# Part of the gate work moved to GpSimd, first loads issued before a branch, and the third weight slice stored as high and low halves

## The chip, the cores and the metric

One core of a Trainium2 chip runs the program. The metric is the device time of one execution in microseconds (us), given as the median of several runs. The engines are TensorE (PE; its weight loads are shown apart as PEld), VectorE (DVE), ScalarE (ACT), GpSimd (POOL) and SyncE (SP, which here only issues DMAs).

## The reference

An mLSTM attention layer (4 batches, 8 heads, 768 steps, 40 values a head) is followed by a feed-forward layer with a rational activation:

```python
m_new = maximum(f + m, i);  f_stab = exp(f + m - m_new);  i_stab = exp(i - m_new)
C = f_stab * C + i_stab * outer(v, k);   n = f_stab * n + i_stab * k
y = sigmoid(o) * (C @ q) / maximum(abs(n . q), 1)          # step by step over 768 steps
x = y as (3072 tokens, 320)
h = x @ w_in                                               # 320 x 2048
P = a0 + a1*h + a2*h^2 + a3*h^3;  Q = 1 + |b0|*|h| + |b1|*h^2
out = (P / (Q + 1e-6)) @ w_out                             # 2048 x 320
```

The weights arrive as float64; everything else is float32.

## The kernel before

**Stages.** The attention is cut into 24 units (`u`) of 128 steps of one batch. Two units give 256 tokens of x, one block (`n`); there are 12 blocks. Each block is multiplied with `w_in`, goes through the activation and is multiplied with `w_out` in 8 feed-forward units (`i`). So that the first weights are enough for some work, the first two blocks are done by halves: units 0 to 3 of both, then 4 to 7 of both.

**Weights.** They come as pairs of 32-bit integers and are decoded on the chip (`split64`, L732), in slices: i0 to i7 (rows 0 to 255 of `w_in`, 512 KB each), o0 to o7 (`w_out`, 640 KB each), and j0, j1 (rows 256 to 319 of `w_in`, the third slice). A slice takes a load on SP (`raw`), a fill of `lo` and a rebase of `z` on ACT, two integer steps on DVE (a sign step and a join, one pair for each slice i or j), a cast to the high half on ACT, and a subtraction on POOL that leaves the low half. The feed-forward matmuls are products of high and low halves: 8 matmuls of 256 columns make one 128-row chunk of h (`f_f1`, tile `ph`), and 12 of 320 columns make a piece of the second product (tile `po`).

**The third slice** has only 64 rows, so its matmul uses two 64-row halves at once. Tile `wj` holds the high half in one set of partitions, and a DMA (`across`, L826, 4 x 128 KB) copies it into the others. Tile `wY` has the low half in partitions 0 to 63 and zeros in 64 to 127, put there by a memset of 64x2048 on POOL. The x tile `xk` has in its fifth part the high half of the last 64 columns of x in the first partitions and the low half in the others.

**Gates.** Before the first unit a small exponential (`early`) gives the first gates. For all later ones, `gate_m` is a running maximum (a scan on DVE), `gate_f` gets it added (32x512, DVE), eight subtractions of 32x128 give `gate_x` (four on POOL, "li", four on DVE, "lx"), and a row of DVE steps of 128x256 (tiles `gate_x` and `gP`) makes the exponential. `squares` (five steps of 128x1 on DVE) prepares the constants of the activation. For each unit, `e` is a scan (DVE), `kp`, `pm` and `tm` are products on POOL, `ab` and `kT` copies on ACT, `qA` a product of 104x512 (on DVE for the first ten units, on POOL afterwards), and `sm` the new state (for the first of each batch a plain copy, on DVE).

**The order.** All steps stand in one list, written out by hand (`ORDER`, L147 on). Each engine's instructions are chained in that order (`_Queue`, L34, so every such instruction shows L34 in the profile); SP's DMAs are chained likewise, and each DMA waits for the one 8 before it. "hot" are 90 matmuls of the identity with itself whose result nobody reads; each shows as two matmuls in the trace. What runs ahead of the list is `_prologue`: it loads a 4-value tensor and decides on it (`_can_square`, `_decide`), and the program branches on that number, so that nothing of the list starts before it.

```python
parts = [
    (w[:, 0, 0], 0), (w[:, 1, 0], 0), (w[:, 0, 1], 1), (w[:, 1, 1], 1),
    (w[:, 0, 0], 2), (w[:, 0, 1], 3), (wX, 4), (wY[:, c * P : (c + 1) * P], 4),
]
```

Of the kernel before, what the change touches and what calls it, by code (L numbers as in the profile page):

```python
# [147 lines left out]
early early.1 le early.2 early.3 hot hot.1 hot.2 hot.3 hot.4 hot.5 hot.6 hot.7 hot.8 hot.9 hot.10 hot.11 hot.12 hot.13  # L148
hot.14 hot.15 hot.16 hot.17 raw_o1 s2_o1 early.4 zero early.5 early.6 early.7 early.8 early.9 early.10 s0_o1.1
early.11 mc early.12 early.13 early.14 early.15 early.16 early.17 eye1 early.20 early.21 gate.2 gate.4 gate.5 li.2 eye  # L150
s0_o1 s1_o1 s3_o1 li.1 hot.18 s1_o1.1 s3_o1.1 lk_0 pf_0 early.18 raw_i6 gate.6 sc_0 hot.19 hot.20 hot.21 raw_o0 hot.22
pa_0 hot.23 s2_i6 hot.24 hot.25 hot.26 hot.27 s2_o0 s0_o0 o0_o1 s1_o0 hot.28 hot.29 zero.2 s3_o0 s0_o0.1 pa_1 s1_o0.1
s3_o0.1 li.3 lv_0 raw_j1 o2_o1 s0_i6 hot.30 hot.31 hot.32 early.19 ogl_4 gate.3 hot.33 hot.34 ogl_2 s1_i6 squares lx.2
raw_i4 o0_o0 hot.35 hot.36 s0_i4 s2_i4 pc_0 kp_0 tk_0 ke_0 pc_1 s0_j1 s1_i4 o2_o0 hot.37 hot.38 zero.3 s3_i4 o0_i4
ek_0 hot.39 hot.40 hot.41 hot.42 hot.43 zero.1 hot.44 hot.45 hot.46 hot.47 lq_0 hot.48 hot.49 hot.50 raw_o5 hot.51
hot.52 hot.53 hot.54 hot.55 hot.56 o2_i4 hot.57 hot.58 hot.59 hot.60 hot.61 s2_j1 s1_j1 s3_i6 raw_i2 lk_1 raw_j0 s0_o5
kp_1 li s3_j1 ogl_0 o0_i6 s0_o5.1 lq_1 s1_o5 lx.1 hot.62 tq_0 hot.63 s2_o5 eq_0 s1_o5.1 hot.64 o0_j1 hot.65 hot.66
pa_2 ogl_3 o2_i6 lx.3 s3_o5.1 s3_o5 o0_o5 S_0 tk_1 hot.67 qa_0 P_0 P_0.1 lx s0_j0 pc_2 ogl_5 raw_i0 ow_0 pf_1 gate.7
u0_0 ek_1 gate.21 lv_1 hot.68 tq_1 s1_j0 o2_j1 hot.69 hot.70 hot.71 d1_0 ogl_1 lk_2 o2_j1.1 sc_1 s2_j0 s3_j0 eq_1
s0_i2 hot.72 hot.73 hot.74 s2_i2 hot.75 S_1 ke_1 qa_1 o2_o5 o0_j0 o2_j0 raw_i3 u1_0 P_1 s1_i2 P_1.1 hot.76 pf_2 s0_i0  # L160
s1_i0 raw_i1 s2_i0 og_0 o2_j0.1 gate.1 ow_1 gate s3_i2 it_0 s3_i0 u0_1 d1_1 it_0.1 i1_0 hot.77 ab_0 ab_0.1 lq_2 hot.78
hot.79 hot.80 hot.81 sc_2 s0_i3 rc_0 kp_2 u1_1 s1_i3 tk_2 hot.82 g_0 x_0 o0_i0 o0_i2 g_0.1 ke_2 s2_i3 s3_i3 x_0.1
hot.83 hot.84 hot.85 hot.86 hot.87 hot.88 hot.89 ek_2 s2_i1 pf_3 s0_i1 s1_i1 s3_i1 xt_0 o2_i0 oc_j0 xh_0 xl_0 tq_2
eq_2 xh_0.1 o0_i1 o0_i3 S_2 lk_3 xl_0.1 raw_o3 lv_2 kp_3 tk_3 f1_0_0 f1_0_0.1 P_2 P_2.1 ek_3 s0_o3 s2_o3 o2_i1 lf_4
lq_3 ow_2 qa_2 sc_3 o2_i2 ha_0_0 s1_o3 s0_o3.1 pa_3 s3_o3 u0_2 d1_2 ke_3 u_0_0 s1_o3.1 s3_o3.1 p1_0_0 p3_0_0 u1_2
w_0_0 tq_3 eq_3 S_3 P_3 y_0_0 r0_0_0 P_3.1 lk_4 f1_0_1 sc_4 kp_4 tk_4 pc_3 raw_o2 gh_0_0 ek_4 m_0_0 oc_j1 f1_0_1.1
f1_0_2 qa_3 s0_o2 s0_o2.1 raw_i7 rm_0_0 s1_o2 s2_o2 ha_0_1 o2_i3 u_0_1 s1_o2.1 p1_0_1 s0_i7 s3_o2 s2_i7 w_0_1 gl_0_0
# [1306 lines left out]
```

## Time and profile before

| | us |
|---|---|
| median of 3 runs | 500.86 |
| the three runs | 499.60, 500.86, 504.22 |
| the profiled execution | 500.23 |
| its span (first to last instruction) | 498.4 |
| time around the span | 1.8 |
| TensorE's granted clock over the span, as a share of full speed | 0.998 |

The profile is of one execution. Its span is what the views of the trace cut up: a page by engine, tables by stretch of time, groups of instructions, waits, the single engines' timelines, and DMA issues. The part around the span is not seen in them.

### The profile page before, as it was taken

The page shows a single profiled execution, that of the slowest core. Times are in us where ns is not written, and L with a number is a line of the kernel's source. Part 1 is how long each engine was busy: PE and PEld are TensorE (multiplying, and loading weights), DVE is VectorE, ACT ScalarE, POOL GpSimd, SP SyncE. Part 2 cuts the span into 40 slices and gives each one's busy share as a digit, 9 for nine tenths or more (in the row PEclk, how much of TensorE's full clock was granted, in tenths as well). Part 3 has the DMA queues.
Part 4 walks back from the last instruction along what each step waited for, and adds up shares of the span by engine and source line. Part 5 has one row for each costly group of instructions (what it writes and reads, how often), then busy time and mean ns, then how long its engine had stood idle before and what let it go on. Part 6 is the DMA issues. An engine that isn't in the chain of part 4 may idle for free.

```text
span 498.4 us, 14219 instructions
## 1 busy us (share of the span) xinstructions
PE 478.1 (96%) x5631; PEld 462.1 (93%) x5631; DVE 421.9 (85%) x716; ACT 402.5 (81%) x698; POOL 385.8 (77%) x365
## 2 busy tenths in 40 slices
...
GB/s 181 221 178 238 229 208 177 103 9 71 113 106 77 59 83 101 99 75 83 44 83 87 131 70 57 60 77 15 29 115 62 2 75 3 11 19 1 27 1 35
DMA packets 120158, 42.54 MB, mean 85 GB/s; under 512 B 104338, under 2 KB 112594, under 8 KB 120082
## 3 DMA queue, kind: packets, MB, share of 16 engines
...
q14 instruction: 30, 0.25, 0.2%
...
## 4 chain that ended last, share of the span: by engine, by line
PE 73%; DVE 7%; ACT 5%; DMA 4%; issue 3%; POOL 3%; SPq 3%; DVEq 0%; ACTq 0%; POOLq 0%
PE ph L34 30%; PE po L34 29%; PE y L34 4%; PE kq L34 3%; PE ow L34 3%; SPq L34 2%; PE ps L34 2%; DMA kr<-in_k_dram 2%; POOL p L34 2%; PE px L34 1%; DMA rawo<-in_moe_w_out_dram 1%; ACT ph L34 1%; DMA rawi<-in_moe_w_in_dram 1%; DVE w L34 1%; DVE gH L34 1%
## 5 line engine op out<-in xcount | busy, mean ns | idle before, releaser
L34 POOL TENSOR_TENSOR p<-p,w 128x512 f32<-128x512 f32 (+1 forms) x97 | 127.8, 1318 | 59.7 <-DVE w L34 55.8
L34 PE MATMUL ph<-xk,wi 128*128 128x256 f32 x1152 | 167.9, 282 | 0.6 <-DVE zo L34 0.5
L34 PEld LDWEIGHTS ph<-xk,wi 128*128 128x128 f32 x1152 | 150.0, 188 | 1.9 <-PE ph L34 0.7
L34 POOL TENSOR_TENSOR w<-w,ha 128x512 f32<-128x512 f32 (+1 forms) x97 | 127.3, 1318 | 9.9 <-ACT w L34 9.9
L34 PE MATMUL po<-wo,gH 128*128 128x320 f32 x768 | 134.6, 312 | 0.0
L34 PEld LDWEIGHTS po<-wo,gH 128*128 128x128 f32 x768 | 115.1, 188 | 0.8
L34 DVE SCALAR_TENSOR_TENSOR gL<-p,ps,ph 128x512 fp32r<-128x512 f32 (+1 forms) x97 | 71.3, 735 | 22.0 <-POOL p L34 19.9
L34 DVE SCALAR_TENSOR_TENSOR w<-w,gH 128x512 f32<-128x512 f32 (+1 forms) x97 | 81.7, 843 | 4.0
L34 ACT ACTIVATE ph<-w,cd 128x512 f32<-128x512 f32 (+1 forms) x97 | 66.6, 687 | 22.6 <-POOL w L34 12.2
L34 DVE SCALAR_TENSOR_TENSOR gH<-p,ps,ph 128x512 fp32r<-128x512 f32 (+1 forms) x97 | 71.3, 735 | 13.8 <-ACT ph L34 12.8
L34 ACT ACTIVATE w<-ha,ba 128x512 f32<-128x512 f32 (+1 forms) x97 | 78.6, 812 | 2.3
L34 ACT ACTIVATE ha<-ph 128x512 f32<-128x512 f32 (+1 forms) x97 | 57.5, 593 | 27.4 <-PE ph L34 26.6
L34 PE MATMUL po<-wo,gL 128*128 128x320 f32 x384 | 77.2, 314 | 0.8 <-DVE gL L34 0.8
L34 DVE SCALAR_TENSOR_TENSOR p<-p,ps,ph 128x512 f32<-128x512 f32 (+1 forms) x97 | 70.5, 734 | 7.2 <-ACT p L34 7.0
L34 ACT ACTIVATE p<-ph,ps 128x512 f32<-128x512 f32 (+1 forms) x97 | 65.3, 680 | 0.3
L34 PEld LDWEIGHTS po<-wo,gL 128*128 128x128 f32 x384 | 59.2, 188 | 2.4 <-DVE gL L34 1.8
L34 ACT ACTIVATE ph<-ph 128x512 f32<-128x512 f32 (+1 forms) x97 | 56.0, 578 | 2.2
L34 PE MATMUL ph<-xk,wY 128*128 128x256 f32 x192 | 53.6, 279 | 0.0
L34 PE MATMUL ph<-xk,wj 128*128 128x256 f32 x192 | 53.4, 278 | 0.0
L34 PEld LDWEIGHTS ph<-xk,wj 128*128 128x128 f32 x192 | 36.2, 188 | 0.0
L34 PEld LDWEIGHTS ph<-xk,wY 128*128 128x128 f32 x192 | 36.1, 188 | 0.0
L34 PE MATMUL hot<-ident 128*128 128x128 f32 x180 | 24.9, 296 | 4.0 <-DVE flag_out L370 4.0
...
## 6 DMA issues: line engine op xcount, KB each, us to landing
...
ab<-scrA SPq DMA_DIRECT2D x40, 128.0 KB, 3.6
...
```

The source lines that it names most:

```text
L34: made = fn(*args, **kwargs)
```

## The change

- `_prologue`: the loads of k, q (on SP's queue) and v (two DMAs, on ACT's queue) of unit 0 are issued there, ahead of the branch, with a new common tile `kr`; a sigmoid of one value on ACT stands there too.
- To POOL: the addition to `gate_f`, the four "lx" subtractions, four of the five steps of `squares` (the reciprocal stays on DVE as "inverse"), the sum that makes `eye1`, the ones of `vb0`, and `qA` of units 0 to 3. The plain state copies of units 0 to 3 go to ACT.
- Third slice: no `across` DMAs, no `wY` and no memset. The low half is written into the other partitions of `wj`. The last 64 columns of x are doubled by a new copy on POOL ("xd", 128x2x64, once a block) and transposed 128 wide; `xk` has six parts, the fifth with the high half and the sixth with the low one, each in all 128 partitions.
- `gt` has two buffers, `z` seven for six.
- `ORDER` is written anew in its first third, up to about block 5; behind that only "xd" is put in.

```diff
+    nc.scalar.activation(c["cd"][0:1, 1:2], c["cd"][0:1, 0:1], AF.Sigmoid)
...
+    nc.sync.dma_start(c["kr"], k)
+    nc.sync.dma_start(c["qn0"][:, :, 0:D], q)
...
-        step(lambda: V.tensor_tensor(gf, gf, gm[:, 0:SR], ALU.add), 0.95, r=["gm"], w=["gA.f"])
+        step(lambda: nc.gpsimd.tensor_tensor(gf, gf, gm[:, 0:SR], op=ALU.add), 1.3, "POOL", r=["gm"], w=["gA.f"])
         for j in range(NQ):
-            plan.add("lx", "DVE", 0.3, lambda j=j: less(V, xf, gf, j), r=["gA.f", "gm"], w=[f"gB.f{j}"])
+            plan.add("lx", "POOL", 0.6, lambda j=j: less(nc.gpsimd, xf, gf, j), r=["gA.f", "gm"], w=[f"gB.f{j}"])
...
-        plan.add(
-            "zero", "POOL", 2.0, lambda: nc.gpsimd.memset(wY[L:P].bitcast(F32), 0.0), w=["wj0.l", "wj1.l"]
-        )
...
-        def across(t):
-            for j in range(2):
-                nc.sync.dma_start(t[rr[1 - j], cols[j]].bitcast(F32), t[rr[j], cols[j]].bitcast(F32))
-
         def low(j, t, z):
-            c = (2 * j + s) * n
-            subtract(wY[0:L, c : c + n], z[rr[j]], t[rr[j], cols[j]])
+            subtract(t[rr[1 - j], cols[j]], z[rr[j]], t[rr[j], cols[j]])
...
-            if u < FIRST:
+            if B <= u < FIRST:
                 nc.vector.tensor_tensor(d["qA"], d["kq"][0:DP].rearrange("p (n c t) -> p n c t", n=NP, c=2), ab, ALU.mult)
             else:
                 nc.gpsimd.tensor_tensor(d["qA"], qT, ab, op=ALU.mult)
...
-                nc.vector.tensor_copy(dst, own)
+                nc.scalar.copy(dst, own)
...
+        def f_xd():
+            nc.gpsimd.tensor_copy(d["xn"][:, :, DM:], d["xn"][:, :, 2 * P : DM])
...
-                nc.vector.tensor_tensor(xt[L:P, 4, tk], pm(x), xt[0:L, 4, tk].bitcast(F32), ALU.subtract)
+                nc.vector.tensor_tensor(xt[:, 5, tk], pm(x), xt[:, 4, tk].bitcast(F32), ALU.subtract)
...
-                (w[:, 0, 0], 2), (w[:, 0, 1], 3), (wX, 4), (wY[:, c * P : (c + 1) * P], 4),
+                (w[:, 0, 0], 2), (w[:, 0, 1], 3), (wX, 4), (wX, 5),
```

SP's queue at the program's start, before (`kr0` is k of unit 0, `raw` are weight slices, `flag_out` the number that is branched on):

```order
L354 DMA flag_a_67<-in_moe_a_dram 1x4
L337 DMA g_63<-in_f_gate_dram 32x256
L337 DMA g_63<-in_i_gate_dram 32x256
L371 TENSOR_LOAD flag_out_70
L319 COMPARE_AND_BRANCH
L34 DMA rawo1_191<-in_moe_w_out_dram 128x2x640
L34 DMA gate_f_155<-in_f_gate_dram 32x512
L34 DMA gate_f_155<-in_i_gate_dram 32x512
L34 DMA kr0_234<-in_k_dram 128x8x40
```

And the same place after:

```order
L361 DMA flag_a_68<-in_moe_a_dram 1x4
L337 DMA g_63<-in_f_gate_dram 32x256
L337 DMA g_63<-in_i_gate_dram 32x256
L347 DMA kr_64<-in_k_dram 128x8x40
L348 DMA qn0_61<-in_q_dram 128x8x40
L378 TENSOR_LOAD flag_out_71
L319 COMPARE_AND_BRANCH
L34 DMA rawo5_165<-in_moe_w_out_dram 128x2x640
L34 DMA rawi4_174<-in_moe_w_in_dram 128x2x512
L34 DMA gate_f_160<-in_f_gate_dram 32x512
```

k and q of unit 0 stand ahead of the branch now, and the first weights directly behind it.

DVE around the subtraction that makes the low half of x (`xk0`), the last DVE step that the first feed-forward matmul waits for; before (`lo0i1`, `zi1` decode slice i1, `pm2` and `qA2` are unit 2's, `e3` unit 3's):

```order
L34 SCALAR_TENSOR_TENSOR lo0i3_714<-rawi3_618,lo0i3_714 128x512
L34 TENSOR_TENSOR xn0_730<-y0_0_666,gt0_0_728 128x4x2x40
L34 SCALAR_TENSOR_TENSOR zi3_740<-zi3_740,lo0i3_714 128x512
L34 TENSOR_TENSOR xn0_730<-y1_0_679,gt0_1_736 128x4x2x40
L34 SCALAR_TENSOR_TENSOR lo0i1_772<-rawi1_645,lo0i1_772 128x512
L34 SCALAR_TENSOR_TENSOR zi1_753<-zi1_753,lo0i1_772 128x512
L34 TENSOR_TENSOR xk0_787<-px0_0_776,xk0_787 128x512
L34 TENSOR_TENSOR xk0_787<-px1_0_777,xk0_787 64x256
L34 TENSOR_TENSOR pm2_738<-ps0_2_801,e2_712 128x4x64
L34 TENSOR_TENSOR pm2_738<-ps1_2_802,e2_712 128x4x64
L34 TENSOR_TENSOR qA2_871<-kq_2_790,ab2_520 104x512
L34 SCALAR_TENSOR_TENSOR e3_873<-fb_3_755,eye_118 128x512
```

And after:

```order
L34 TENSOR_TENSOR pm2_618<-ps0_2_647,e2_546 128x4x64
L34 TENSOR_TENSOR pm2_618<-ps1_2_648,e2_546 128x4x64
L34 TENSOR_TENSOR xn0_688<-y0_0_565,gt0_0_686 128x4x2x40
L34 TENSOR_TENSOR xn0_688<-y1_0_591,gt0_1_690 128x4x2x40
L34 SCALAR_TENSOR_TENSOR lo0i0_681<-rawi0_679,lo0i0_681 128x512
L34 SCALAR_TENSOR_TENSOR gP_490<-gP_490,gate_x_161 128x256
L34 SCALAR_TENSOR_TENSOR zi0_683<-zi0_683,lo0i0_681 128x512
L34 SCALAR_TENSOR_TENSOR e3_741<-fb_3_724,eye_124 128x512
L34 SCALAR_TENSOR_TENSOR lo0i1_745<-rawi1_743,lo0i1_745 128x512
L34 SCALAR_TENSOR_TENSOR zi1_775<-zi1_775,lo0i1_745 128x512
L34 TENSOR_TENSOR xk0_780<-px0_0_759,xk0_780 128x512
L34 TENSOR_TENSOR xk0_780<-px1_0_760,xk0_780 128x256
```

Slices i3, i2 and i6 are decoded behind `xk0` now, and steps of the gate exponential (`gP`), unit 3's scan and unit 2's `pm` ahead of it.

PE around the first feed-forward matmul (`ph0_0_0`), before (`hot` is the matmul of the identity, `kq` and `pa` are transposes and copies of the attention, `px` those of x):

```order
L34 MATMUL hot_172<-ident_58 128x128 x8
L34 MATMUL fb_3_755<-g_63,ident_58 64x64 x16
L34 MATMUL px0_0_776<-ident_58,xn0_730 128x128 x4
L34 MATMUL px1_0_777<-ident_58,xn0_730 64x128 x2
L34 MATMUL kq_2_790<-ident_58,qn0_61 104x128 x4
...
L34 MATMUL kq_3_827<-ident_58,kp_60 104x128 x4
L34 MATMUL ph0_0_0_832<-xk0_787,wi0_732 128x256 x6
L34 MATMUL ph0_0_0_832<-xk0_787,wj0_614 128x256
L34 MATMUL ph0_0_0_832<-xk0_787,wY_138 128x256
```

And after, up to the second chunk:

```order
L34 MATMUL px1_0_760<-ident_58,xn0_688 128x128 x2
L34 MATMUL hot_186<-ident_58 128x128 x5
L34 MATMUL kq_3_801<-ident_58,qn1_132 104x128 x4
L34 MATMUL hot_186<-ident_58 128x128 x4
L34 MATMUL ph0_0_0_812<-xk0_780,wi0_772 128x256 x6
L34 MATMUL ph0_0_0_812<-xk0_780,wj0_550 128x256 x2
...
L34 MATMUL hot_186<-ident_58 128x128 x6
L34 MATMUL ow_2_896<-vb0_62,pm2_618 64x82 x8
L34 MATMUL hot_186<-ident_58 128x128 x2
L34 MATMUL ph0_1_0_912<-xk0_780,wi1_799 128x256 x6
```

Before, all 90 "hot" stand ahead of the first feed-forward matmul; after, 59 do and 31 stand behind it, spread over the first block and the start of the second.

## Rows read from the trace of the kernel before

**Rows 1.** The page, part 1: busy time, share of the span, instructions.

```profile
PE 478.1 (96%) x5631; PEld 462.1 (93%) x5631; DVE 421.9 (85%) x716; ACT 402.5 (81%) x698; POOL 385.8 (77%) x365
```

**Rows 2.** Stretches: length; busy PE, PEld, DVE, ACT, POOL; granted clock, DMA share, GB/s.

```profile
11.00:50.40 39.40, 34.92 (x593) 32.21 (x594) 32.81 (x66) 30.27 (x56) 26.03 (x31) 1.00 0.98 218
50.40:100.00 49.60, 45.46 (x644) 42.01 (x641) 48.50 (x97) 45.27 (x83) 42.15 (x40) 1.00 0.92 178
100.00:135.00 35.00, 35.00 (x398) 34.31 (x399) 32.53 (x56) 31.99 (x59) 31.02 (x27) 1.00 0.31 63
```

**Rows 3.** PE's waits from 100 to 490 us: total, times, longest (us).

```profile
PE po L34 <- DVE gL L34: 0.8, 2, 0.4
```

**Rows 4.** PE's timeline up to 60 us: start, length (us), instruction, count.

```profile
3.97 6.77 PE L34 MATMUL hot<-ident 128*128 128x128 f32 x38 [3.97 <-DVE flag_out L370]
...
19.58 5.97 PE L34 MATMUL hot<-ident 128*128 128x128 f32 x52
...
50.41 0.94 PE L34 MATMUL ph<-xk,wi 128*128 128x256 f32 x6
...
53.03 1.10 PE L34 MATMUL pa<-g,ident 128*64 128x64 f32 x32
54.06 0.65 PE L34 MATMUL kq<-ident,qn 128*104 128x128 f32 x4
```

**Rows 5.** Groups of DVE instructions from 4 to 50.4 us: busy us, mean ns.

```profile
L34 DVE SCALAR_TENSOR_TENSOR lo0i<-rawi,lo0i 128x512 int32<-128x512 int32 x6 | 4.1, 691 | 2.6 <-ACT lo0i L34 2.6
L34 DVE SCALAR_TENSOR_TENSOR zi<-zi,lo0i 128x512 int32<-128x512 int32 x6 | 4.0, 684 | 0.5 <-ACT zi L34 0.3
L34 DVE TENSOR_TENSOR_SCAN e<-fb,eye 128x512 f32<-128x512 f32 x3 | 3.6, 1210 | 0.0
...
L34 DVE TENSOR_TENSOR pm<-ps,e 128x256 f32<-128x256 f32 x5 | 2.0, 420 | 0.0
L34 DVE SCALAR_TENSOR_TENSOR ps<-pa,ps 128x1 f32<-128x1 f32 x1 | 1.5, 1523 | 0.0
...
L34 DVE TENSOR_TENSOR gate_f<-gate_f,gate_m 32x512 f32<-32x512 f32 x1 | 0.7, 671 | 0.0
L34 DVE COPY sm<-ow 104x164 f32<-104x164 f32 x2 | 0.6, 322 | 0.0
```

**Rows 6.** Timeline of DVE and POOL around 30 us: start, length (us).

```profile
30.21 1.27 POOL L34 TENSOR_TENSOR wi<-zi,wi 128x512 fp32r<-128x512 f32 x1
...
30.40 2.46 DVE L34 TENSOR_TENSOR gate_x<-gate_f,gate_m 32x128 f32<-32x128 f32 x1
...
31.45 1.26 POOL L34 TENSOR_TENSOR wY<-zj,wj 64x512 fp32r<-64x512 f32 x1
```

**Rows 7.** Instructions on tile qA: ns least/median/most, first and last start.

```profile
L34 POOL TENSOR_TENSOR qA<-qT,ab x14: 1277/1296/1751, 176.1 to 437.0; 104x512 f32<-104x512 f32 x14
L34 DVE TENSOR_TENSOR qA<-kq,ab x10: 658/683/692, 29.1 to 148.1; 104x512 f32<-104x512 f32 x10
```

**Rows 8.** Instructions on tile gate_x, columns as in rows 7.

```profile
L34 DVE SCALAR_TENSOR_TENSOR gP<-gP,gate_x x5: 419/420/432, 84.4 to 91.0; 128x256 f32<-128x256 f32 x5
L34 POOL TENSOR_TENSOR gate_x<-gate_f,gate_m x4: 402/407/663, 12.8 to 29.8; 32x128 f32<-32x128 f32 x4
L34 DVE TENSOR_TENSOR gate_x<-gate_f,gate_m x4: 282/284/2460, 21.5 to 30.4; 32x128 f32<-32x128 f32 x4
```

**Rows 9.** Groups of POOL instructions up to 100 us: busy us, mean ns.

```profile
L34 POOL TENSOR_TENSOR wi<-zi,wi 128x512 fp32r<-128x512 f32 x8 | 10.3, 1299 | 2.2 <-ACT wi L34 2.2
...
L34 POOL TENSOR_TENSOR wY<-zj,wj 64x512 fp32r<-64x512 f32 x4 | 5.1, 1264 | 0.2
...
L34 POOL MEMSET wY<- 64x2048 f32 x1 | 1.8, 1801 | 0.1
```

**Rows 10.** DMA up to 100 us: the busiest queue's share, and one group of issues.

```profile
q1 hardware_dynamic: 43378, 18.92, 89.1%
...
wj<-wj SPq DMA_DIRECT2D x4, 128.0 KB, 4.9
```

More of the change, by code (lines that the diff above doesn't have):

```diff
@@ L147 @@
 ORDER = """
[L148 to L167, printed above, removed]
@@ L339, in _prologue @@
         )
+    nc.vector.memset(c["vb0"], 0.0)
     nc.vector.memset(c["kp"], 0.0)
-    nc.vector.memset(c["vb0"], 0.0)
     make_identity(nc, c["ident"])
     nc.gpsimd.memset(c["cd"][:, 0:1], CD)
+    nc.scalar.activation(c["cd"][0:1, 1:2], c["cd"][0:1, 0:1], AF.Sigmoid)
     nc.gpsimd.memset(c["qn0"], 0.0)
+    q, k, v = (x[0, :, 0:P].rearrange("h t d -> t h d") for x in args[0:3])
+    nc.sync.dma_start(c["kr"], k)
+    nc.sync.dma_start(c["qn0"][:, :, 0:D], q)
+    for j in range(2):
+        r = slice(j * L, (j + 1) * L)
+        nc.scalar.dma_start(c["vb0"][r, :, j, 0:D], v[r])
     return c
@@ L650, in gates @@
         early()
-        plan.add("eye1", "DVE", 0.2, lambda: eyes1(), w=["eye1"], new=[("eye1", ("gt", 1))])
+        plan.add("eye1", "POOL", 0.2, lambda: eyes1(), w=["eye1"], new=[("eye1", ("gt", BUFS["gt"]))])
         plan.add("eye", "ACT", 0.62, eyes, r=["eye1"], w=["eye"])
@@ L664, in gates @@
         if square:
-            plan.add("squares", "DVE", 1.2, squares, r=["pab"], w=["ps"])
+            plan.add("inverse", "DVE", 0.2, lambda: V.reciprocal(ps[:, 3:4], pa[:, 3:4]), r=["pab"], w=["ps"])
+            plan.add("squares", "POOL", 1.2, squares, r=["pab"], w=["ps"])
         step(turn, 0.35, "PE", r=xis, w=["pi"], new=[("pi", ("h", BANKS))])
@@ L775, in add @@
             plan.add(f"{op}_{name}", *args, **kw)
-        many = 2 if across else 1
+        many = 2 if apart else 1
         add("raw", "SP", 1.46 * c, load, w=[raw], lag=plan.DMA)
@@ L785, in split64 @@
         add("o0", "ACT", 0.5 * c * many, high_part, r=zz, w=[out])
-        if across:
-            add("oc", "SP", 1.2, lambda: across(wt[name]), r=[out], w=[f"{out}.x"], lag=plan.DMA)
         for j in range(len(low)):
@@ L1056, in attention @@
         add("ow", "PE", 0.85, f_ow, r=["pm.1", "pm.00", "pm.01", V], w=["ow"], new=new("ow"))
-        add("u0", "DVE", 0.66, lambda: update(0, s), r=["t0"] if later else [], w=["ow", *SM])
+        add("u0", "DVE" if later else "ACT", 0.66, lambda: update(0, s), r=["t0"] if later else [], w=["ow", *SM])
         add("d1", "POOL", 0.74, lambda: decay(1, s), r=[*SM, "ab"], w=["t1"], new=[("t1", ("tm1", 1))])
```

339 lines of the change are left out of this document (181 added, 158 removed).

## The prediction

> **What bounds the kernel now.** I read the page first: PE is busy 478.1 of 498.4 us, DVE, the next, 421.9 [rows 1]. Shares of a whole span hide stages, so the second view is the table by stretch, and the third PE's waits. From 100 to 490 us PE waits twice, 0.8 us in all [rows 3]: there PE alone sets the time, and an engine made lighter gives nothing. PE's work in that part is the same before and after: the transposes of x stream the same 128 columns, and a chunk of h is still 8 matmuls of 256. So all that the change can give lies ahead of 100 us. The first feed-forward matmul starts at 50.41 us [rows 4]. From 11 us to there DVE is busy 32.81 of 39.40 us, POOL 26.03 and the DMA share is 0.98; from there to 100 us DVE is busy 48.50 of 49.60 and PE 45.46 [rows 2]. PE's 34.92 us in the first of the two stretches [rows 2] are mostly the "hot" matmuls, which compute nothing: 52 of them took 5.97 us [rows 4], 115 ns each, and a step of the list is two, 0.23 us. The time is therefore three terms: when the first feed-forward matmul starts, how long the stretch behind it lasts until PE is full, and a rest that stays.
>
> **Term 1, the start of the feed-forward work.** It waits for x (a DVE chain), for the first slices (DMA, ACT, DVE, POOL) and for the third slice.
>
> DVE ahead of the last subtraction on `xk0`, by the order and the rows. What goes: the addition to `gate_f`, 0.67 [rows 5]; four subtractions of `gate_x`, three at 0.284 and one of 2.46, 3.3 in all [rows 8]; four steps of `squares`, one of them 1.52 [rows 5] and three of some 0.2, 2.1; two copies `sm`, 0.64 [rows 5]; two `qA`, 1.37 [rows 7]; the sum for `eye1`, about 0.2. That makes 8.3. The decoding of i2, i3 and i6 goes behind it: 0.691 + 0.684 a slice [rows 5], 4.1. What comes ahead of it instead: ten steps of the gate exponential at 0.42 [rows 8], 4.2; unit 3's scan, 1.21; unit 2's two `pm` at 0.42 [rows 5], 0.84; 6.3 in all. Net: 8.3 + 4.1 - 6.3 = 6.1 us less.
>
> Loads: k and q are issued before the branch instead of 5 to 18 us into the span, and up to the last o-gate load of the first block SP issues 5568 KB where it issued 7104 (counted from the order; 480 KB of the new sum are k, q and v of unit 0, in flight while the branch is decided). At 218 GB/s [rows 2] 7104 - 5088 KB are 9.2 us. With the queue at 89.1% of the DMA engines [rows 10], that is a gain on a resource that is full, and the four copies of 128 KB within SBUF that stood among the loads [rows 10] go too.
>
> POOL ahead of it gets 4 x 0.41 for `gate_x` [rows 8], two `qA` at 1.30 [rows 7] and the addition to `gate_f`. That one no row shows on POOL: at the least a `gate_x` of a quarter its size, 0.41 [rows 8], at the most twice its DVE time, as `qA` has it, 1.3; I take 1.3, since `qA` is nearer in size. The four steps of `squares` there are bounded by 0.41 each from above and by nothing from below; I take 0.1 each, as they have one value a partition. It loses a memset of 1.80 [rows 9] and the decoding of a slice. Sum: about 4 us more, in a stretch where it idles 13 of 39.4 [rows 2]. Covered, unless the extra work falls where a unit waits for its `kp` or `pm`.
>
> DVE's 6.1 would be the gain if DVE alone led, the loads' 9.2 if they did. Walking along the chain of the first two units with these durations, the start comes out at 42.6 to 44. I take 43.4: -7.0 us.
>
> **Term 2, the stretch until PE is full.** The order shows that 31 "hot" now stand behind the first feed-forward matmul: 31 x 0.23 = 7.1 us of PE. Unit 3's `pa` and one set of `kq` move ahead of it, about 1.0 us after their overlap [rows 4]. PE had 49.60 - 45.46 = 4.1 us free in this stretch [rows 2]. So PE's own need there becomes 45.5 + 7.1 - 1.0 = 51.6, against a stretch of 49.6: it can't shrink below that, and it grows by 2.0 us even with no wait left. The others: DVE -3.7 by the order (two `qA`, two `sm` and the gate steps that went ahead, against the three slices that came), ACT some +3.5, POOL +7.7 (two `qA` at 1.30, two `wi` at 1.30, two halves of wj at 1.26 [rows 7, 9]), which had 7.5 us free there and 4.0 in the next 35 [rows 2]. All four engines then want 45 to 52 us. Before, the stretch was 1.1 longer than its fullest engine; PE's busy time counts modelled ends of lone matmuls, so its true need is somewhat below 51.6. Least: 0 (a "hot" put exactly into waits that stay). Most: +6.1 (all 7.1 paid, the free 4.1 as before). I take +2.4.
>
> **Term 3, the rest.** "xd" is new on POOL, 12 times. No row shows it; it is 128x128 values: a quarter of a `wi` makes 0.32 [rows 9], a whole one 1.30, and I take 0.45, nearer the quarter. It lies between `xn` and the transposes of x, and after 100 us PE has other work in the list meanwhile: 0. If that cover were gone, 11 x 0.45 = 5 us. Ahead of 50 us it is in the walk. The second half of the x casts goes from 64 to 128 partitions with the same length a partition: 0. `gt` and `z` with one buffer more: 0 or a little gain.
>
> **Sum.** 500.23 for the profiled execution, -7.0, +2.4: 495.6 us. The median of the runs is 0.63 above that execution, so against 500.86 this is 5.2 less, 1.0%. About 1%, 5.0 us, is what a measurement of this kernel can tell from no change.
>
> **A rule that speaks against it.** One subtraction `gate_x` on DVE took 2.46 us and began beside a POOL subtraction and ended within the next one, where its median is 0.284 [rows 6, 8]. The Trainium skill, page "SBUF — State Buffer", section "SBUF: two separate sides", says that a GpSimd instruction and a DVE instruction with two SBUF inputs exclude each other for the whole instruction on a shared port pair. The trace agrees for this one pair; by the rule the gain of the small steps is partly that they no longer queue behind POOL, but each microsecond more of POOL work is one in which such a DVE step may stand. That is the last rival below.
>
> **Rivals.**
> Faster: the loads lead and DVE's shorter chain lets them, so the start gains 9.2, and the "hot" fill only waits that stay, +0. 500.23 - 9.2 = 491.0. For it: a DMA share of 0.98 up to the start [rows 2]. Against it: PE's need above.
>
> Nothing gained: the list moves the "hot", not the work. Start -7.0, stretch +6.1, since the 4.1 us of waits are those for DVE and ACT and stay where they are: 499.3. For it: DVE 48.50 busy of 49.60 [rows 2] means that the waits were for it, and four engines near 50 us don't interlock without loss. Against it: DVE loses 3.7 there. A milder form ends here too: with 59 "hot" for 90 ahead, TensorE's clock could fall to the lower of its two levels (1.2 for 2.4 GHz) while the attention's small matmuls run. The stretch before shows 1.00 granted throughout [rows 2], but the first 38 "hot" took 178 ns each, where later ones took 115 [rows 4], so the engine's pace isn't a constant there. A start four us later would be 499.6.
>
> Slower: POOL becomes what holds DVE. Place: from 11 us to PE's saturation. POOL's extra work is 4 us ahead of the start and 7.7 behind it. If DVE's steps stand still for all of it, the start gains only 3.0 and the stretch grows by 2.4 + 7.7: 500.23 - 3.0 + 10.1 = 507.3. It is slower than before from some 45% of those 11.7 us on. For it: the 2.46 us. Against it: of four such subtractions one was hit, and many of the DVE steps there have an operand in PSUM.
>
> **How the numbers follow.** The forecast's case has a chance of 0.52, by itself 492.5 to 498.5 (start 42.6 to 44.4, stretch +0.5 to +4): a good half of it is faster than 495.85. The faster rival has 0.19, the one with nothing gained 0.20, the slower one 0.09. Faster by over 1%: 0.27 + 0.19 = 0.46. Within 1%: 0.25 + 0.20 = 0.45. Slower by over 1%: 0.09. The range goes from below the faster rival, 489.5, past the case of nothing gained to 502.0, where half of the POOL rival begins.
>
> **What would show it.** In the changed kernel's trace: the first `ph` matmul at 43 to 44 us; PE without waits from about 95 us on; 62 "hot" entries behind that start, and PE's busy time up to saturation as long as the stretch; DVE busy under 47 us there; no subtraction of `gate_x` on DVE, and POOL's eight at about 0.4 us. I am wrong in term 1 if the start isn't within a microsecond and a half of 43.4, in term 2 if the time between that start and PE's saturation has shrunk, and in term 3 if PE waits for `px` or `xk` behind 100 us.

## The result, and the profile after

The changed kernel takes 506.4 us (median of 11 runs, 504.5 to 509.48), the kernel before, run beside it, 501.6 (11 runs): a ratio of 1.0087 [1.0066, 1.0108]. It is slower by 0.9%; the medians differ by 4.8 us. That is 10.8 us above the forecast of 495.6 and above the end of its range, 502.0.

One caution on the two profiles. The profiled execution of after took 509.48 us, the longest of its 11, and that of before 500.23, among the shortest: they lie 9.3 us apart where the medians lie 4.8 apart. The traces tell where time goes; what it is worth is taken from the medians.

The page of the changed kernel, part 1 (busy time, share of the span of 507.7 us, instructions), against [rows 1]:

```profile
PE 481.5 (95%) x5631; PEld 464.7 (92%) x5631; DVE 419.8 (83%) x696; ACT 403.5 (79%) x702; POOL 397.8 (78%) x392
```

DVE gave up 2.1 us, POOL took 12.0, PE is busy 3.4 us longer with the same number of matmuls. Nothing here says what went wrong. The stretches do, with the columns of [rows 2]:

```profile
11.00:50.40 39.40, 33.64 (x578) 31.24 (x579) 27.59 (x59) 26.58 (x52) 27.25 (x39) 0.91 0.83 192
50.40:100.00 49.60, 47.32 (x627) 45.25 (x626) 46.00 (x86) 46.74 (x87) 43.92 (x42) 1.00 0.71 170
100.00:135.00 35.00, 34.77 (x331) 33.65 (x330) 32.72 (x51) 31.38 (x55) 30.37 (x26) 1.00 0.44 75
```

In the first stretch DVE is busy 5.2 us less (6.1 were forecast), but the DMA share fell to 0.83 and the granted clock to 0.91: the DMA engines that were to be full are not, and something stood still. From 100 to 135 us PE is busy 34.77 of 35.00 and yet did 331 matmuls where it did 398 before. The mix of long and short ones differs too, so that alone proves nothing; it is a reason not to take a busy PE for one that gets on.

PE's timeline of after:

```profile
37.42 1.07 PE L34 MATMUL kq<-ident,qn 128*104 128x128 f32 x4 [4.70 <-DVE ba L34]
...
42.05 2.69 PE L34 MATMUL hot<-ident 128*128 128x128 f32 x18
...
51.58 0.96 PE L34 MATMUL ph<-xk,wi 128*128 128x256 f32 x6
```

The feed-forward work starts at 51.58 us, 1.2 later than in [rows 4], not 7.0 earlier. PE stood for 4.70 us in one piece just before 37.4, in front of the transposes of unit 2's q. ACT's waits up to 100 us, and the chain that ended last up to 51.6 us (start, length, what), say for what:

```profile
ACT lo0j L34 <- DMA rawj<-in_moe_w_in_dram: 3.0, 1, 3.0
```

```profile
29.89 5.06 DMA rawj<-in_moe_w_in_dram
...
35.05 0.64 ACT lo0j L34
...
35.72 0.70 DVE lo0j L34
...
36.66 0.68 DVE zj L34
...
37.42 1.07 PE kq L34 x4
```

The load of the third slice's second half (j1) lands at 35.0 us, ACT stood 3.0 us for it, and its decoding on ACT and DVE stands in their queues ahead of what PE needs next. ACT has a longer wait, 9.4 us for its first slice of `w_in`, but it is not on this chain: it ended at 11.6 us, and held up the gates of unit 0 (`inat`) by 0.9 us at the most.

Behind 100 us the view of waits shows little (PE, 100 to 490 us: total, times, longest; against [rows 3]):

```profile
PE kq L34 <- DVE gL L34: 1.0, 1, 1.0
```

That is the longest of five, 2.6 us in all.

The page's part 4, the chain that ended last by engine, shows more; before and after:

```profile
PE 73%; DVE 7%; ACT 5%; DMA 4%; issue 3%; POOL 3%; SPq 3%; DVEq 0%; ACTq 0%; POOLq 0%
```

```profile
PE 60%; DVE 13%; POOL 11%; ACT 5%; issue 5%; DMA 4%; SPq 1%; DVEq 0%; POOLq 0%; ACTq 0%
```

PE gave up 13% of the span in this chain, DVE and POOL took 14% more. To see where, I read a lap time off PE's timeline: the start of the first transpose of x in each of the 12 blocks (x0 to x11). Two of these rows from before, then the same two from after:

```profile
108.45 0.82 PE L34 MATMUL px<-ident,xn 128*128 128x128 f32 x6
...
209.30 0.82 PE L34 MATMUL px<-ident,xn 128*128 128x128 f32 x6
```

```profile
112.34 0.82 PE L34 MATMUL px<-ident,xn 128*128 128x128 f32 x6
...
216.70 0.82 PE L34 MATMUL px<-ident,xn 128*128 128x128 f32 x6
```

Block x2 is 3.89 us late, x5 is 7.40. The table has these lags for the profiled execution of each kernel whose trace is read so below (us behind before; x0 of before is at 47.25). A lag that stays the same from one column to the next means that the stretch took as long as before. The first column varies under one and the same list: four kernels that are alike up to there (after, hots_out, splice, new_late) have it from -3.6 to +1.3. The steps between columns are what an edit does to the stretch. In new_late and old_late the edit moves these transposes themselves back in the list, so their columns hold a part that is the mark's own.

| | x0 | x1 | x2 | x3 | x5 | x7 | x9 | x10 | x11 |
|---|---|---|---|---|---|---|---|---|---|
| after | +1.3 | +4.1 | +3.9 | +5.2 | +7.4 | +7.8 | +8.1 | +8.0 | +8.1 |
| hots_out | -0.3 | +1.8 | +2.8 | +4.1 | +6.2 | +6.6 | +6.9 | +7.0 | +7.1 |
| both_nohot | -2.9 | +3.6 | +5.1 | +6.5 | +8.7 | +9.0 | +9.2 | +9.2 | +9.2 |
| splice | -3.6 | -0.8 | +2.3 | +2.4 | +3.0 | +3.5 | +3.7 | +3.6 | +3.7 |
| old_list | +0.7 | +2.5 | +3.6 | +3.6 | +4.3 | +4.7 | +5.0 | +4.9 | +4.9 |
| old_dve | +0.8 | +1.8 | +5.2 | +5.2 | +5.9 | +6.4 | +6.6 | +6.5 | +6.6 |
| old_xd_dve | -1.6 | -0.7 | -0.0 | -0.0 | +0.6 | +2.2 | +2.4 | +2.9 | +3.1 |
| new_xd_dve | -1.5 | +2.4 | +2.6 | +4.0 | +6.9 | +8.5 | +8.8 | +9.3 | +9.5 |
| old_noslice | +2.2 | +2.9 | +5.0 | +5.0 | +5.0 | +5.0 | +5.0 | +5.2 | +5.2 |
| old_split | +0.5 | +1.0 | +1.4 | +2.3 | +2.3 | +2.3 | +2.6 | +2.6 | +2.5 |
| loads_only | -1.2 | -1.4 | -1.4 | -1.4 | -1.4 | -1.4 | -1.4 | -1.4 | -1.4 |
| loads_gates | +2.1 | +2.0 | +1.9 | +1.9 | +1.9 | +1.9 | +1.9 | +1.9 | +1.9 |
| loads_xd | -2.7 | -1.3 | +0.6 | +0.6 | +1.2 | +1.5 | +1.8 | +1.8 | +1.7 |
| loads_xd_late | -0.2 | -0.4 | -0.5 | -0.5 | -0.5 | -0.5 | -0.5 | -0.5 | -0.6 |
| loads_xd_act | -4.2 | -0.2 | +1.9 | +1.9 | +1.9 | +3.5 | +5.2 | +5.3 | +5.4 |
| new_late | -1.1 | +1.6 | +1.7 | +3.1 | +8.2 | +9.5 | +9.5 | +19.3 | +18.1 |
| old_late | -0.7 | -1.3 | -0.7 | -0.7 | -0.6 | +0.6 | +0.6 | +9.6 | +8.4 |

So after loses 6.1 us between x0 and x5 (47 to 217 us), and 0.7 in all the rest. The 1.2 that is missing to its span lies behind x11.

### The profile page after: what moved, and what is told of

It reads as the page before. It is cut to its first block, busy times and chain, and to the rows that moved or that the text cites. A ratio compares the mean times of both kernels' runs of the same rounds, so it can differ in the third digit from the quotient of the medians.

```text
span 507.7 us, 14220 instructions
## 1 busy us (share of the span) xinstructions
PE 481.5 (95%) x5631; PEld 464.7 (92%) x5631; DVE 419.8 (83%) x696; ACT 403.5 (79%) x702; POOL 397.8 (78%) x392
## 4 chain that ended last, share of the span: by engine, by line
PE 60%; DVE 13%; POOL 11%; ACT 5%; issue 5%; DMA 4%; SPq 1%; DVEq 0%; POOLq 0%; ACTq 0%
PE ph L34 24%; PE po L34 23%; POOL p L34 4%; PE kq L34 3%; DVE w L34 3%; PE y L34 3%; POOL w L34 3%; PE ow L34 2%; PE ps L34 2%; DVE gH L34 2%; ACT ph L34 2%; DVE p L34 1%; DMA scrF<-g 1%; SPq L34 1%; DVE gL L34 1%
## 5 line engine op out<-in xcount | busy, mean ns | idle before, releaser
L34 DVE SCALAR_TENSOR_TENSOR w<-w,gH 128x512 f32<-128x512 f32 (+1 forms) x97 | 86.6, 892 | 4.6 <-POOL p L34 0.5
L34 PE MATMUL ph<-xk,wj 128*128 128x256 f32 x384 | 75.6, 278 | 0.0
L34 PEld LDWEIGHTS ph<-xk,wj 128*128 128x128 f32 x384 | 58.2, 188 | 0.0
L34 PE MATMUL hot<-ident 128*128 128x128 f32 x180 | 28.8, 313 | 4.0 <-DVE flag_out L377 4.0
L34 PEld LDWEIGHTS hot<-ident 128*128 128x128 f32 x180 | 25.9, 223 | 4.8 <-issue 4.0
L34 POOL TENSOR_TENSOR kp<-kr,inat 128x320 f32<-128x320 f32 x24 | 21.5, 898 | 6.0 <-ACT inat L34 5.5
```

Source lines behind the costliest of these rows:

```text
L34: made = fn(*args, **kwargs)
```

## The experiments

Ratios are to the kernel before on the same chip, with a 95% interval. Where two kernels were not run side by side, their ratios are divided.

**The start.** Four runs take away what the trace showed ahead of and behind the first feed-forward matmul. hots_out takes the 31 "hot" out that stand behind it:

```diff
-HOT = 90
+HOT = 59
```

> The changed kernel without the 31 hot steps that stand behind the first feed-forward matmul (59 stay). Theory H, they are paid in full because PE has next to no free time there: 31 x 0.23 = 7.1 us less than the changed kernel, about 499.3 us, a ratio to before of 0.995. Rival F, they only fill waits: within 2 us of the changed kernel, 505 to 507, ratio 1.009. Rival C, they hold up the granted clock: the clock falls behind the start and the time is not shorter.

Measured: 507.72 us, 1.0105 [1.006, 1.0149]. Taking the late "hot" out gains nothing: they filled waits that stay. From x0 to x2 the kernel loses 3.1 us without them, 2.6 with them. That they cost nothing is not shown, as the clock changed too: from 52 to 60 us PE is busy 5.62 us in hots_out at a granted clock of 0.79, 6.82 us in after at 1.00 (rival C of the expectation, not tested apart).

q2_early issues unit 2's load of q (`lq_2`) 70 steps earlier in the list, and j1_later does the decoding of slice j1 behind unit 2's products:

```diff
-... ke_2 gate.21 inverse lq_2 tq_2 ab_0 ...
+... s3_o1.1 hot.20 lq_2 raw_j0 ...
```

```diff
-... u1_1 raw_j1 s0_j1 s1_j1 gate.13 s2_j1 s3_j1 it_0.1 ...
+... P_2 P_2.1 s0_j1 s1_j1 s2_j1 s3_j1 og_0 hot.35 ...
```

> The changed kernel with one load moved in the list: q of unit 2 ahead of the loads of j0. PE stood still from 32.7 to 37.4 us before unit 2's q transposes. Theory Q, the load of q was late: the 4.7 us go, the clock stays up in what follows, and the time falls by 3 to 6 us to 500 to 503. Rival J, PE waited for DVE, which stood behind the decoding of slice j1: the wait stays and the time is within 2 us of 506.

> The changed kernel with the four decoding steps of slice j1 moved behind unit 2's pm, the load of j1 where it was. Theory J, ACT and DVE stood still for j1's load (3.0 and 3.5 us) with all that is queued behind, PE's 4.7 us among it: the wait goes and the time falls by 3 to 6 us to 500 to 503. Rival Q, the q load was late: PE still waits until 37 us and the time is within 2 us of 506. If the start of the feed-forward work is set by slice i0's load (issued at 35.2 us), both this and q2_early free the wait and the time still stays within 2 us of 506.

Measured: 509.06 us, 1.0146 [1.0104, 1.0188], and 510.11, 1.0151 [1.0107, 1.0196]. Neither helps; each is 0.6% behind after. The first `ph` came at 51.05 and 51.11 us. Each edit leaves the other wait: in j1_later PE still stands 3.6 us for the load of q, in q2_early 3.8 us a little later, behind the decoding of j1.

both_nohot has all three edits.

> The three edits together: no late hot steps, q of unit 2 early, j1 decoded later. If H holds and one of Q and J, the terms add up: 506.4 - 7.1 - 4 = about 495, ratio 0.988. If only H holds: 499. If neither: 506. The start of the feed-forward work should come at 46 to 48 us for 51.6 if the waits set it, at 51 if the load of slice i0 does.

Measured: 510.29 us, 1.016 [1.0118, 1.0203]. With both waits gone its first `ph` came at 47.36 us, 4.2 earlier than in after, and the gain is gone by the next block: x0 is 2.9 us ahead of before, x1 3.6 behind. An earlier start alone shortens nothing here. As the late "hot" are out as well, the clock has a part in it: from 48 to 56 us PE is busy 3.46 of 8, and from 56 to 60 the granted clock is 0.50.

**The parts, one at a time.** old_list has every part of the change under the list of before (with "xd" and "inverse" put in, the memset and `across` left out):

> All parts of the change with the list of before (the copies of wj and the memset of wY taken out of it, each xd put in behind its x, inverse ahead of squares). Theory L, the rewritten list is what costs, since PE did 5.2 us less useful work from 50 to 100 us and 4.4 us less from 100 to 250 us: the parts by themselves cost nothing and this kernel takes 498 to 502 us, a ratio to before of 0.99 to 1.00. Rival P, the parts cost, POOL's additional work above all: 505 to 508, as with the new list.

Measured: 506.32 us, 1.0076 [1.0053, 1.01], as slow as after. The new list is not needed for the loss.

old_dve is old_list with the gate steps, `squares`, `eye1`, `qA` and the state copies back on DVE, so that the early loads and the third slice remain; loads_only has the early loads (and the early sigmoid) alone:

```diff
-                nc.scalar.copy(dst, own)
+                nc.vector.tensor_copy(dst, own)
...
-            plan.add("lx", "POOL", 0.6, lambda j=j: less(nc.gpsimd, xf, gf, j), r=["gA.f", "gm"], w=[f"gB.f{j}"])
+            plan.add("lx", "DVE", 0.3, lambda j=j: less(V, xf, gf, j), r=["gA.f", "gm"], w=[f"gB.f{j}"])
```

> The list of before, the early loads and the new third slice, but the gate steps, eye1, the ones of vb0, the state copies and qA of units 0 to 3 on DVE as before. Against old_list this is the move to POOL and ACT alone. Theory L: the same as old_list within 2 us, or slower by up to 6 us if DVE leads in the old list. Rival P: 4 to 6 us faster than old_list.

> The kernel before with one part, k, q and v of unit 0 loaded ahead of the branch and the early sigmoid. In the old list k of unit 0 was issued at 5.6 us and v at 7.9 us, and PE filled the time with hot: by theory L the start moves by less than 2 us and the time is 500 to 502. If the loads led the start, 3 to 5 us less, 497.

Measured: old_dve 506.38 us, 1.0075 [1.0048, 1.0101]; loads_only 499.62, 0.9954 [0.9917, 0.999]. The early loads gain half a per cent and beat both kernels. Between the two lies the third slice with its buffers: 1.0075 / 0.9954, 1.2%.

splice has after's list up to the chunk `f1_1_3` of the second block and that of before behind it:

> The changed kernel with its own list up to the fourth chunk of the second block (about 100 us) and, for all that is left, the order of before. Theory L with the loss in two places: what it lost up to 100 us stays, about 3.6 us of PE's work, and the 4.4 us from 100 to 250 us go: 502 ratio 1.000 to 1.003 (against 506.4). If all is lost up to 100 us: 506.

Measured: 505.33 us, 1.0079 [1.0046, 1.0111]. With the first part of the new list the time is that of either whole list.

**The doubling of x.** old_xd_dve and new_xd_dve put "xd" on DVE, under either list:

```diff
-            nc.gpsimd.tensor_copy(d["xn"][:, :, DM:], d["xn"][:, :, 2 * P : DM])
+            nc.vector.tensor_copy(d["xn"][:, :, DM:], d["xn"][:, :, 2 * P : DM])
```

> old_list with one edit: the copy xd on DVE, directly behind the two x that it reads, where it waits for no other engine. With it on POOL, POOL stood still for DVE's x 6.6 us in 6 waits behind 100 us and 4.3 us in 3 waits from 44 to 120 us, with the feed-forward products queued behind. Theory X, that wait is what the new third slice costs (old_dve has everything of loads_only but the slice, and takes 6.8 us more): 499 to 502 us, ratio 0.995 to 1.000. Rival Y, the slice costs by something else (the wider x tile, seven z buffers, the tile layout): 505 to 507.

> The changed kernel with xd on DVE at its place in the new list. Theory X: 3 to 6 us less than the changed kernel, 500 to 503 us. Rival Y: 506 within 2 us. If the new list has a loss of its own beside xd, it ends between: 503 to 505.

Measured: 505.77 us, 1.008 [1.0039, 1.0121], and 511.02, 1.0157 [1.0126, 1.0189]. Moving it away from POOL doesn't help, though in old_xd_dve no engine but DVE has to wait for x: there the lag grows by 2.3 us from x0 to x5, for 3.6 in old_list, and by 2.5 behind x5, for 0.6. So the wait on POOL is not all that the copy costs. The copy itself, in old_xd_dve, then on POOL in after (ns least/median/most, first and last start):

```profile
L34 DVE COPY xn<-xn x12: 226/774/1149, 44.8 to 451.9; 128x128 f32<-128x128 f32 x12
```

```profile
L34 POOL COPY xn<-xn x12: 288/488/1222, 43.8 to 457.0; 128x128 f32<-128x128 f32 x12
```

old_noslice is old_list with the third slice as it was before (`wY`, memset, `across`, no "xd"), so that the early loads and the moves to POOL and ACT remain:

> The list of before with the early loads and the moves to POOL and ACT, and the third slice as before (copies of wj by DMA, wY and its memset, no xd; six z and one gt). Theory X and rival Y alike, if the slice is the only part that costs: as loads_only, 499 to 501 us, or some us less if taking 8 us of work off DVE ahead of the start is worth anything in the old list. If the moves to POOL cost too: 503 or more.

Measured: 503.25 us, 1.0011 [0.9988, 1.0035]. The moves cost 1.0011 / 0.9954, 0.6%. In the table they cost 0.7 us from x0 to x1, 2.1 from x1 to x2 and 0.2 in the rest. On top of the moves the slice costs 1.0076 / 1.0011, 0.6%; on top of the slice (old_dve) the moves cost nothing.

loads_xd asks what "xd" costs by itself. It is loads_only with a copy of 128x2x32 on POOL at the place of "xd", into a tile that nobody reads:

```diff
+        def f_xd():
+            flat = d["xn"].rearrange("p c h d -> p c (h d)")
+            nc.gpsimd.tensor_copy(ap1.tile([P, 2, L // 2], F32, tag="xd", name=f"xd{m}"), flat[:, :, 2 * P : 2 * P + L // 2])
...
+        add("xd", "POOL", 0.3, f_xd, r=[f"xnat{m}.0", f"xnat{m}.1"], w=[f"xdat{m}"])
```

> loads_only with a copy on POOL behind every x that reads x and whose result (128x2x32 values) nobody uses; nothing else waits for it. Theory X: POOL's wait for DVE's x alone, 3 to 6 us more than loads_only, 503 to 506. If what costs in xd is that the transposes of x wait for it, or if rival Y holds: 499 to 501, as loads_only.

Measured: 505.53 us, 1.0065 [1.0036, 1.0095]. Twelve copies of 0.24 us (238 ns in the median), whose result nobody waits for, cost 1.0065 / 0.9954, 1.1%, some 5.5 us.

**The copy or the wait for x.** loads_xd_late has the same copy three POOL products later in the list, loads_xd_act has it at the old place, on ACT:

```diff
-... s3_i3 x_0.1 xd_0 hot.83 ...  eq_4 x_1.1 xd_1 rm_0_1 ...
+... s2_o3 o2_i1 xd_0 lf_4 ...  lf_5 kp_5 xd_1 d0_4 ...
```

```diff
-        add("xd", "POOL", 0.3, f_xd, r=[f"xnat{m}.0", f"xnat{m}.1"], w=[f"xdat{m}"])
+        add("xd", "ACT", 0.3, f_xd, r=[f"xnat{m}.0", f"xnat{m}.1"], w=[f"xdat{m}"])
```

> loads_xd with the unused copy three POOL products further back in POOL's queue, where its x is long written. Theory W, POOL's wait for DVE's x is the price of xd: as loads_only, 499 to 501 us, and the 7.1 us of waits for xn on POOL are gone. Rival T, POOL's own time for the copy and what it does to the rest of the list is the price: 503 to 506, as loads_xd (505.5).

> loads_xd with the unused copy on ACT, at the same place, directly behind x. Theory W in its general form, any engine that stands still for DVE's x there passes the wait on: 503 to 506. If only POOL's queue is that tight (POOL and DVE hand w and p to each other): 499 to 501.

Measured: loads_xd_late 500.73 us, 0.9973 [0.9941, 1.0005]; loads_xd_act 506.06, 1.0078 [1.0045, 1.0111]. The same instruction on the same engine costs 0.9% more (1.0065 / 0.9973, 4.6 us) where it stands for x. On ACT, where POOL does nothing for it, it costs as much as on POOL. The view of the copy's tile gives its length (ns) and, below, how long its engine stood in front of it, in how many pieces; loads_xd, then loads_xd_act:

```profile
L34 POOL COPY xd<-xn x12: 233/238/708, 43.9 to 450.5; 128x64 f32<-128x64 f32 x12
...
  DVE xn L34: 7.1, 7
```

```profile
L34 ACT COPY xd<-xn x12: 228/245/248, 43.0 to 454.1; 128x64 f32<-128x64 f32 x12
...
  DVE xn L34: 11.1, 7
```

In loads_xd_late the copies take 0.24 us as well, and POOL stands in front of none. So in this list the wait is the price, not the copy. The chain that ended last shows it for POOL, from 71 to 110 us (start, length, what). First loads_xd_late:

```profile
89.07 2.36 PE y L34 x96
91.43 0.50 PE po L34 x2
91.92 1.89 PE ph L34 x16
...
95.72 2.90 PE ph L34 x24
```

And loads_xd:

```profile
88.91 2.43 PE y L34 x96
...
92.25 0.76 DVE gH L34
...
93.81 2.14 POOL p L34
95.95 0.69 POOL gt L34
96.64 1.70 issue
98.36 0.24 POOL xd L34
98.59 0.69 POOL pm L34
...
105.67 0.76 DVE gL L34
...
106.47 0.85 PE po L34 x4
```

Where the copy stands late, the chain is PE's own from matmul to matmul. Where it stands early, the chain leaves PE at 91.3 us and comes back at 106.5; from the `y` at 89 us to the transposes of x2, loads_xd takes 1.2 us longer. The piece to look at is the 1.70, which POOL's timeline (start, length, in brackets the idle time ahead) names:

```profile
95.91 0.73 POOL L34 TENSOR_TENSOR gt<-og,na 128x320 f32<-128x320 f32 x1
98.36 0.24 POOL L34 COPY xd<-xn 128x64 f32<-128x64 f32 x1 [1.72 <-DVE xn L34]
```

POOL has finished `gt`, DVE has still to multiply x with it (`xn`), behind two other steps in its own queue, and POOL stands until then, because the next instruction in its queue is the copy of that x. Behind it stand `pm`, `w` and `p`, for which PE and DVE wait. From x0 to x2 loads_xd loses 3.2 us, from x2 to x11 1.1. It started 2.7 us ahead of before; whether a part of the 3.2 is a lead that would have gone in any case is not shown. Nor is the way of ACT's wait: in loads_xd_act the chain from 75 us to 109 us is PE's.

old_split has the third slice without "xd": the transposes stay 64 wide, and ACT and DVE write the halves of x into both sets of partitions, each with two instructions:

```diff
-            nc.scalar.copy(xk[nb][:, 0:2, tk] if x == 0 else xk[nb][:, 4, tk], pm(x))
+                for r in (slice(0, L), slice(L, P)):
+                    nc.scalar.copy(xk[nb][r, 4, tk], pm(x))
...
-                nc.vector.tensor_tensor(xt[:, 5, tk], pm(x), xt[:, 4, tk].bitcast(F32), ALU.subtract)
+                for r in (slice(0, L), slice(L, P)):
+                    nc.vector.tensor_tensor(xt[r, 5, tk], pm(x), xt[0:L, 4, tk].bitcast(F32), ALU.subtract)
```

> old_dve without xd: x isn't doubled, the last 64 columns are transposed 64 wide as before, and ACT and DVE write the high and the low part twice, once for each half of the partitions (one 64x256 cast and one 64x256 subtraction more a block, 0.37 and 0.42 us). So the new third slice without its copy. Theory X, xd is what the slice costs: 499 to 502 us. Rival Y, the slice costs by something else: 505 to 507, as old_dve (506.4).

Measured: 503.65 us, 1.0022 [0.9989, 1.0055]. Against loads_only that is still 0.7%, against old_dve 0.5% less. Nearly half of the slice's 1.2% goes with "xd"; whether the rest is the second writes, which only this form has, or the slice or its buffers (`z`, `gt`), which both have, is not settled.

loads_gates is loads_only with the small gate steps on POOL, but `qA` and the state copies left on DVE:

> old_noslice with qA of units 0 to 3 and the state copies on DVE as before, so loads_only and the small gate steps on POOL alone. old_noslice took 503.25 us and loads_only 499.6. If the gate steps on POOL are what costs: 502 to 504. If qA on POOL is: 499 to 500.5, or less, since DVE loses 6 us of work and waiting ahead of the start.

Measured: 501.14 us, 0.9975 [0.995, 1.0001]. The interval overlaps that of loads_only, and the table has no loss behind x0. So by the medians the larger part of the moves' 0.6% belongs to the others, `qA` on POOL and the copies on ACT, which were not tried apart.

**Moving "xd" itself.** new_late (after's kernel, blocks 4 to 11) and old_late (old_dve, all blocks) have "xd" two POOL products later, and the transposes of x, which need it here, behind it:

```diff
-... f2_4_5 x_6.1 xd_6 xt_6 gh_4_6 ... ha_5_0 f1_5_1 p1_5_0 xl_6 p3_4_7 rm_4_6 w_4_7 ...
+... f2_4_5 x_6.1 gh_4_6 ... ha_5_0 f1_5_1 p1_5_0 p3_4_7 rm_4_6 xd_6 xt_6 xh_6 xl_6 w_4_7 ...
```

> The changed kernel with xd of blocks 4 to 11 two POOL products further back in the list, and the transposes of x behind it (in blocks 0 to 3 the new list already has products between). Theory W: POOL's waits for xn behind 100 us (4.8 us in 5 times) go, and the time falls by 2 to 4 us, to 502 to 504. If the later transposes cost as much as the wait did, or if what the changed kernel loses lies ahead of 100 us: 505 to 507.

> old_dve (early loads, new slice, all gate steps on DVE, list of before) with every xd two POOL products further back and the transposes of x behind it. Theory W: what loads_xd_late gave back, 0.9%, so 506.4 - 4.5 = 502, ratio 1.000; it can't beat loads_only unless the slice's saved DMA, memset and weights are worth more than the rest of its cost. If the slice costs by more than the wait (old_split says 0.7% over loads_only): 502 to 504.

Measured: 520.85 us, 1.0343 [1.0307, 1.038], and 512.35, 1.0196 [1.016, 1.0231]. PE's waits from 100 to 490 us, of new_late, then of old_late:

```profile
PE px L34 <- POOL xn L34: 8.4, 3, 3.7
```

```profile
PE px L34 <- POOL xn L34: 6.1, 2, 3.7
```

In old_late the lag is flat up to x5, where old_dve's had grown by 5.1 us, so with the late copy the slice costs nothing there. Between the marks of x9 and x10 it jumps by 9.0: at 377 us PE has stood 3.7 us for the late copy, and a part of the jump is the moved mark. The two waits make 6.1 of the 11.2 us by which old_late's profiled execution is longer than that of before; the rest is not traced. The wait can't simply be moved: at the early place POOL pays it, at this one PE.

## Why the prediction was wrong

**Term 1, the start: 7.0 us forecast, none or little came.** The step that failed is "7104 - 5088 KB are 9.2 us", together with the walk along the chain that took it up. It priced the loads by their sum, as if the start waited for all of them at the rate of [rows 2]. In the changed kernel the DMA share up to 50.4 us is 0.83, so the engines have room; what is waited for is single loads: j1's, with its decoding in the order of ACT and DVE, and unit 2's q. With both waits taken away (both_nohot) the start came at 47.36 us, still 4.0 behind 43.4. The start also differs between kernels with the list of after unchanged up to there: the first `ph` came at 51.58 (after), 49.95 (hots_out), 49.14 (new_late) and 46.70 us (splice), against 50.41 before; never within 1.5 us of 43.4, which is the bound that the prediction set itself. PE's wait in front of unit 2's q transposes was 4.7, 3.2, 3.2 and 1.9 us in these four. And the start was not the lever that it was taken for. The three kernels of the table that start 2.9 to 4.2 us ahead of before (both_nohot, splice, loads_xd_act) are all 1.9 us or more behind it at x2. Of the kernels that start ahead, loads_only and loads_xd_late kept their lead to the end; behind x0 they are as before. The costs of the single gate steps were right meanwhile; POOL's eight in after, against [rows 8]:

```profile
L34 POOL TENSOR_TENSOR gate_x<-gate_f,gate_m x8: 400/406/407, 15.3 to 24.2; 32x128 f32<-32x128 f32 x8
```

DVE was relieved nearly as forecast. It was not what held the start. POOL's sum ahead of the start, "about 4 us more", is 2.8 from the prediction's own rows (1.64 + 2.60 + 1.30 + 0.40, less 1.80 and a `wi` of 1.30); up to 50.4 us POOL was busy 1.2 us more.

**Term 2, the stretch up to saturation: +2.4 forecast.** In the profile, x0 to x2 is 2.6 us longer, a fit of the number alone. The step "PE's own need there becomes 51.6" is not borne out: with the 31 "hot" taken out (hots_out) the stretch loses 3.1 and the time doesn't fall. They went into waits that stayed, the prediction's lower end for them, with the clock as the part that is open. What made the stretch longer is no need of PE: the chain that ended last (after, 60 to 112 us) runs over POOL's own products from 70.9 to 91.7 us, with 2.7 us of "issue" in it, where that of before is PE's from 79.6 us on.

```profile
70.94 1.05 POOL p L34
...
84.75 1.26 POOL p L34
...
90.44 1.26 POOL w L34
...
91.72 0.70 ACT ph L34
```

No run takes this work off POOL under the new list, so that it is the price there is read from the trace and not shown by an experiment.

**Term 3, the rest: 0 forecast.** "xd" was walked ahead of 50 us and taken as covered behind 100; block 1, whose x comes at 72 us, lies between and was priced by neither. And the cover asked whether PE has other work, not what POOL would stand for. Under the list of before that is a real price: in old_list POOL stands for `xn` 9.2 us in 8 pieces, 5.0 of them up to x5, where old_list loses 3.6. By the medians the wait of the unused copy alone is 4.6 us (loads_xd against loads_xd_late): the prediction's price without cover, "11 x 0.45 = 5 us", is near in size, but it counted the length of the copies, where what costs is the standing still. Its own copy took 0.49 us in the median for the 0.45 assumed.

In the changed kernel itself this wait is not where the time went. POOL stands 1.9 us in front of the copy at 43.8 us and 0.6 in front of the one at 174, but not in blocks 1, 2 and 3; of block 1, on POOL's timeline:

```profile
72.16 0.29 POOL L34 COPY xn<-xn 128x128 f32<-128x128 f32 x1
```

The other 4.2 of its 6.6 us lie behind x5, where after loses 0.7. So the two lists lose the same by the medians, but not in the same way, and for the new one the cause is open.

The reasoning above it failed as well: "there PE alone sets the time, and an engine made lighter gives nothing", read from PE's two waits [rows 3]. It holds from x5 on: from there to x11 after loses 0.7 us and no other kernel with "xd" on POOL at its place more than 1. From 100 to 210 us it doesn't. With after's list the lag grows by 3.5 us from x2 to x5, and the chain there (after, 136 to 172 us) leaves PE:

```profile
138.79 0.74 PE ow L34 x16
...
141.25 1.22 DVE e L34
...
144.64 1.42 POOL gt L34 x2
146.07 0.70 ACT ph L34
...
152.21 0.74 DVE gL L34
153.00 0.64 PE kq L34 x4
```

For 14 us the end is set by DVE, POOL and ACT in turn, while PE counts as busy for 13.24 of them (same stretch, columns as in [rows 2]):

```profile
138.80:153.00 14.20, 13.24 (x220) 12.69 (x221) 12.87 (x24) 12.38 (x21) 11.25 (x12) 1.00 0.48 101
```

With the list of before (old_list) that growth is 0.7 us, yet the two medians are equal, so what that growth is worth is open: after's profiled execution is its longest. That PE would wait for `px` or `xk` behind 100 us, the mark that the prediction named for this error, didn't show in after: the error showed in the chain.

**The sum by the medians.** Early loads -0.5%, the moves +0.6%, the third slice +1.2%; that would be 1.3%, and all together measure 0.8 to 0.9%. They don't add, as the moves cost nothing on top of the slice; that both lengthen the same waits is a guess.

**The rivals.** Nothing gained, 499.3, had the right idea, that a head start is given back up to saturation, but put it down to the "hot". The slower one, 507.3, has the size that came. Its place, POOL between the start and saturation, is where after's chain runs; its reason, POOL standing in DVE's way, is not borne out as the price. DVE's `w` steps did take 86.6 us in after for 81.7 before, but 3.7 of those 4.9 us lie behind 217 us, where after loses 0.7. loads_gates puts the small steps on POOL at a loss of 0.2% that its interval doesn't tell from none, and loads_xd_act has the loss of an early copy with POOL out of it. The one row that spoke for this rival was also read slightly wrong: the subtraction of 2.46 us [rows 6] ended 0.15 us behind the second POOL instruction, not within it.

**The version to keep** is loads_only, 0.9954 [0.9917, 0.999], 1.3% below after (0.9954 / 1.0087). Its gain is small and barely clear of noise. Open are what the loss is made of under the new list, the rest of the slice's price without "xd", which of `qA` and the copies makes the moves' 0.6%, and what lets the start differ by 5 us under one list.
